# When a spectral filter is loaded: 18 transfers, three places in the row loop, and a zeroing write that holds some of them back

## Chip, core and metric

The kernel runs on one core of a Trainium2 chip. The metric is the device time in microseconds (us) of one execution of the whole kernel. Before the change it was 339.54 us, the median of three runs (339.13 to 340.23).

## What is computed

A block of two residual parts, forward and backward, in one kernel: x is 2048 x 448 (sequence x features) in bf16.

```
h   = x + irfft2( rfft2(LN(x)) * (w_r + i*w_i) )            # w_r, w_i: 2048 x 225
h2  = h + transpose( gelu( LN(LN(h))^T w1 + b1 ) w2 + b2 )  # w1: 2048 x 1792, w2: 1792 x 2048
out = h2, and the gradients of x, w_r, w_i, w1, b1, w2, b2 for a given grad_out
```

The Fourier transforms are matrix products with sine and cosine tables that the kernel makes itself. The change touches only the way in which w_r and w_i come into SBUF (on-chip memory) in the forward part, and a few neighbours of those loads.

## The kernel before

**Engines and order.** PE (TensorE) does all products; DVE (VectorE) and ACT (ScalarE) empty PSUM and do the elementwise work; POOL (GpSimd) does small statistics; SP (SyncE) does nothing but start transfers. The orders of PE, DVE, ACT and SP are those in which the Python code issues; POOL's order is chosen by a scheduler. Every engine works its own queue strictly in order: an instruction that waits holds all that is queued behind it. SP, ACT and POOL can start transfers. Eight completion counters serve the transfers of SP and ACT in turn, so a start also waits until the transfer eight starts earlier has landed.

**Row stage** (lines 932 to 979, about 16 to 43 us of the span). A loop of 16 row steps t. In step t PE does `row_a(t + 1)` (first transform of one row group: it reads the scaled table `Rs` that `scale_R` makes on DVE from 1/std of the row, and the folded input that `fold_prep` or `fold_quarters` makes on DVE), then `row_b(t - 3)` (second transform). Between them `fill(n)` puts n products of another task on PE, `dg_gen`: 14 column blocks j of grad_out times turned w2 (`w2T`), 16 products each, needed much later. So PE nearly always has work. 1/std comes from `newton_gp` (line 407), ten tiny POOL instructions for a pair of rows, in steps 0, 1, 3, 5 and 7. Sine tables come from `gen_UV`: its Python pieces are called by `uv_step` in steps 1, 2, 4, 5, 7, 9 and 10; the last piece corrects `Vt` (two DVE instructions). From step 11 on PE turns `Ut` and `Vt` in four portions (`gen_inv_s`, line 530).

**Row moves** (line 697). After each second `row_b` a transfer carries two finished rows to `D2`, eight in all; I number them move 1 to 8. SP starts 1 to 7, ACT the eighth. The next stage begins with products that read moves 1, 3, 5 and 7.

**Turned tiles** (line 312). w2 blocks j = 5 to 13 come as transposing transfers from SP, each when a buffer of `w2T_ring` is free: four in the row stage, and five held back (`held_w2`, `CAP`) until after it.

**Filter loads** (`w_io`, line 579). Nine transfers each for w_r and w_i. Per part, moves[0, 2, 4, 6] bring 16 long runs of 7200 bytes, moves[1, 3, 5, 7] bring runs of 450 bytes in reversed order (256 of them, in the first 240), and moves[8] 16 runs of 450 bytes. `w_loads` is a generator; `W_AT` says how many loads each row step pulls: two in each of steps 0 to 5, six in step 6. All of w_r and the five short-run loads of w_i go by SP; the four long-run loads of w_i go by POOL (`late`), each behind a write of one zero by DVE (line 596), which keeps the scheduler from starting it earlier.

**Stage s2** (line 704). Four sets. Each is transformed along the sequence with `Vt`, `Ut`, `Un`, multiplied on DVE with its part of W (`w_mult`, line 753; this reads all 18 loads), transformed back and moved by line 740 to `D3`. Then `inv_rows` reads `D3` and the table `RTm`, which `gen_RT` (line 525) makes with one product and one copy.

**Between the row stage and s2** (lines 984 to 994): `gen_inv_d` twice, three small bias transfers from SP (`load_biases`), the held turned tiles, `gen_RT`, and 17 products of `dg_gen` in three fills.

Of the kernel before, what the change touches and what calls it, by code (L numbers as in the profile page):

```python
# [103 lines left out]
class Ring:  # L104
# [7 lines left out]
    def next(self):  # L112
        v = self.views[self.i % len(self.views)]
        self.i += 1
        Ring.release(v)
        return v
# [8 lines left out]
def kernel(  # L125
# [20 lines left out]
    nc = tc.nc  # L146
# [4 lines left out]
    gp_ = nc.gpsimd  # L151
# [12 lines left out]
    def cut(reg, off, *dims):  # L164
        n = int(np.prod(dims))
        v = reg[:, off:off + n]
        if len(dims) == 1:
            return v
        names = "abcd"[:len(dims)]
        return v.rearrange("p (" + " ".join(names) + ") -> p " + " ".join(names),  # L170
                           **{c: d for c, d in zip(names, dims)})
# [5 lines left out]
    def ps_ff(parts=P):  # L177
        return psum.tile([P, 512], F32, tag="ff", bufs=4, name="ps_ff")
# [5 lines left out]
    def evac(out, in_, scale=None):  # L184
        n = int(np.prod(in_.shape[1:]))
        if load[0] + sc.cost('copy', n, False) <= load[1] + ve.cost('tensor_copy', n, in_.dtype == BF16):
            if scale is None:
                sc.copy(out=out, in_=in_)
            else:
                sc.activation(out=out, in_=in_, func=ACT.Copy, scale=scale)  # L190
        elif scale is None:
            ve.tensor_copy(out=out, in_=in_)
        else:
            ve.tensor_scalar(out=out, in0=in_, scalar1=scale, scalar2=None, op0=ALU.mult)
# [24 lines left out]
    def mm(out, lhsT, rhs, start, stop):  # L219
        nc.tensor.matmul(out, lhsT=lhsT, rhs=rhs, start=start, stop=stop)  # L220
        clock[0] += int(np.prod(rhs.shape[1:])) / 2400.0
        run_due()
# [80 lines left out]
    def load_w2T():  # L303
        j = w2T_ring.i
        if j == NFB:
            return
        wT = w2T_ring.next()
        w2Ts[j] = wT
        if j < N_NAT:
            nc.sync.dma_start(out=w2n[j], in_=B_w2[j * P:(j + 1) * P, :].rearrange("f (t c) -> f t c", c=P))  # L310
            return
        nc.sync.dma_start_transpose(out=wT, in_=B_w2[j * P:(j + 1) * P, :].rearrange("f (t c) -> f t c", c=P))
# [94 lines left out]
    def newton_gp(v, y, sl):  # L407
        vi, yi = nt_i[:, 0, sl], y.bitcast(I32)
        a = nt_f[:, 0, sl]
        gp_.tensor_scalar(out=v, in0=v, scalar1=LN_EPS, scalar2=None, op0=ALU.add)  # L410
        gp_.tensor_scalar(out=yi, in0=v.bitcast(I32), scalar1=-0.5, scalar2=RSQRT_MAGIC, op0=ALU.mult, op1=ALU.add)
        for c0, c1 in RSQRT_STEPS:
            gp_.tensor_tensor(out=a, in0=y, in1=y, op=ALU.mult)
            gp_.tensor_tensor(out=a, in0=a, in1=v, op=ALU.mult)
            gp_.tensor_scalar(out=a, in0=a, scalar1=c0, scalar2=c1, op0=ALU.mult, op1=ALU.add)
            gp_.tensor_tensor(out=y, in0=a, in1=y, op=ALU.mult)
# [108 lines left out]
    def gen_RT():  # L525
        pt = ps_ff()
        mm(pt[:, 0:P], lhsT=Rp, rhs=ident[:], start=True, stop=True)
        evac(out=RTm[:], in_=pt[:, 0:P])
# [47 lines left out]
    Wc = cut(rW, 0, 2, NG, DF)  # L576
    W = Wc.rearrange("p c g k -> p g c k")

    def w_io(dr, di, store):
        Wq = Wc.rearrange("(q s) c g k -> s q c g k", s=2)  # L580
        for c_, d in ((0, dr), (1, di)):
            moves = []
            for i in range(4):
                moves.append((Wq[0][16 * i:16 * i + 16, c_].rearrange("l g k -> l (g k)"), 16 * i, [[P * DF, 16], [1, 16 * DF]]))
                g0 = 0 if i else 1
                moves.append((Wq[1][16 * i:16 * i + 16, c_, g0:NG, :], P - 16 * i - g0,
                              [[P * DF, 16], [-DF, NG - g0], [1, DF]]))
            moves.append((Wq[1][0:16, c_, 0, :], 64, [[P * DF, 16], [1, DF]]))
            late = [m for n, m in enumerate(moves) if n in (0, 2, 4, 6)] if c_ and not store else []
            early = moves if not late else [m for n, m in enumerate(moves) if n not in (0, 2, 4, 6)]  # L590
            for n, (sb, row, dims) in enumerate(early + late):
                d_ap = bass.AP(d.tensor, d.offset + row * DF, dims)
                eng = nc.sync if n < len(early) else gp_
                if eng is gp_:
                    i = 32 * (n - len(early))
                    nc.vector.memset(Wc[i:i + 1, 1, 8, 0:1], 0.0)
                eng.dma_start(out=d_ap if store else sb, in_=sb if store else d_ap)
                yield

# [21 lines left out]
    def scale_R(t):  # L621
        v = Rs_ring.next()
        ve.tensor_scalar(out=v, in0=Rm[:], scalar1=rstd_x[:, t:t + 1], scalar2=None, op0=ALU.mult)
        return v
# [176 lines left out]
    def fill(n):  # L801
        while n > 0 and pending:
            try:
                next(pending[0])
                n -= 1
                if row_ops:
                    row_ops.pop(0)()
            except StopIteration:
                pending.pop(0)
# [12 lines left out]
    def load_biases():  # L822
        gp_.memset(smr, 0.0)
        nc.sync.dma_start(out=gtail[:, 0:64], in_=grad_out[0][S - 16:S, 3 * P:D])
        nc.sync.dma_start(out=smr[0:NFB, 0, :], in_=B_b1.rearrange("(j p) -> j p", p=P))
        nc.sync.dma_start(out=smr[:, 1, :], in_=B_b2.rearrange("(j p) -> j p", p=P))

        def turn():
            for i, dst in ((0, b1col), (1, b2col)):
                nc.sync.dma_start_transpose(out=smc[:, i, :], in_=smr[:, i, :])  # L830

        def place():
            for i, dst in ((0, b1col), (1, b2col)):
                ve.tensor_copy(out=dst[:], in_=smc[:, i, :])
        return turn, place
# [85 lines left out]
    GROUPS = {0: (6, 8), 1: (8, 10), 3: (10, 12), 5: (12, 14), 7: (14, 16)}  # L921
    STATS = {0: (6, 7), 1: (8, 9), **{t: (t + 8,) for t in range(2, 8)}}
    INV_S = {11: 0, 12: 1, 13: 2, 14: 3}
    W_AT = {**{t: 2 for t in range(6)}, 6: 6}
    FILL_A = (4, 4, 8, 12, 6, 3, 3, 4, 5, 3, 3, 2, 2, 2, 3, 3)
    FILL_B = (0, 0, 2, 2, 2, 2, 4, 4, 3, 2, 2, 2, 2, 2, 2, 2)
    def uv_step():
# [4 lines left out]
    for t in range(NT):  # L932
        if t == 0:
            load_w2T()
        if 4 <= t + 1 < NT:
            row_a(t + 1, Rs.pop(t + 1), sc.copy if t == 7 else None)
        if t == 7:
            late_c.pop()()
        fill(FILL_A[t])
        if 3 <= t and t + 3 < NT:  # L940
            if t + 3 in (4, 8, 12):
                while Meter.side:
                    Meter.side.pop(0)()
            Rs[t + 3] = scale_R(t + 3)
        row_b(t - 3, csQ if t - 3 >= 4 * U_Q else None)
        if t == NT - 1:
            for i in range(t - 2, NT):
                row_b(i, csQ)
        if t % 2 and t < 12:
            if t == 1:  # L950
                pass
            elif t // 2 + 2 < 2 * U_Q:
                fold_prep(xn, t // 2 + 2)
            else:
                fold_quarters(xn, t // 2 + 2, t // 2 % 2 * 2)
        if t == 4:
            for w in range(2):
                gp_.tensor_copy(out=csQ[:, w, :, :], in_=csF[:, w, 0, :].rearrange("p (j e) -> p e j", e=2))
        if t == 1:
            while cs_ops:  # L960
                cs_ops.pop(0)()
            uv_step()
        for i in STATS.get(t, ()):
            ln_stats(xn, i, mvx)
        if t in (2, 4, 5, 7, 9, 10):
            uv_step()
        if t in GROUPS:
            a, b = GROUPS[t]
            newton_gp(mvx[:, a:b, 1], rstd_x[:, a:b], slice(a, b))
        for _ in range(W_AT.get(t, 0)):  # L970
            next(w_loads, None)
        if t in INV_S:
            gen_inv_s(INV_S[t])
        if t == 13:
            for c in range(2):
                for e in range(2):
                    sc.copy(out=Rp.rearrange("p (e a q b c) -> p c e a q b", e=2, c=2, q=8, a=2)[:, c, e],
                            in_=Rm[:, 64 * c + 32 * e:64 * c + 32 * e + 32].rearrange("p (q a b) -> p a q b", q=8, a=2))
        fill(FILL_B[t])
# [5 lines left out]
    gen_inv_d(0)  # L985
    fill(6)
    gen_inv_d(1)
    turn_biases, place_biases = load_biases()
    cap[0] = NFB
    while held_w2:  # L990
        held_w2.pop(0)()
    fill(4)
    gen_RT()
    fill(7)

    def fwd_mult(s, j, x, y):
# [1 line left out]

    s2_stage(lambda s: set_of(Xs, s), fwd_mult, 8, (8,) * 5, 0, split=True)
    sc.activation(out=warm, in_=eps_h, func=ACT.Sqrt)  # L1000
    fill(21)

    w1c_ring = Ring([cut(r, o, NT, 256) for r, o in ((r2, 0), (r2, NT * 256), (rO, S))])
# [479 lines left out]
```

## Time and profile before

| What | us |
|---|---|
| median of three runs | 339.54 |
| profiled execution, whole | 340.34 |
| its span | 338.3 |
| PE busy in the span | 330.2 |
| idle time of PE that is put down to a wait for another engine or transfer, the 1.2 us at the start included | 4.2 |
| row stage and what follows up to the first product of s2 | 16 to 48.4 |
| s2 | 48.4 to 75.4 |

The profile is of one execution. A wait is named after the engine or the transfer that ended it. `SPq` and `ACTq` are the queues that start transfers; the time of such a row is the time of starting, not of the data. Where I speak of the landing of one transfer, it is the last count of its completion counter in the trace.

### The profile page before, as it was taken

Reading aid. Unit: us, or ns where it says so; the run is one execution under the profiler, and the core shown is the slowest. Engines: PE = TensorE matmul, PEld = TensorE weight load, DVE = VectorE, ACT = ScalarE, POOL = GpSimd, SP = SyncE. Lnnn points to the kernel's source line nnn. Section 1 sums busy time; section 2 is a strip of 40 time slices with the busy share of each in tenths; the row PEclk is TensorE's granted clock in tenths of the full one; section 3 lists DMA queues with packets and bytes.
Section 4 is the critical chain, followed back from the end, with each engine's and each line's share of the span. In section 5 each row is a group of like instructions: output and inputs, shape, how many; then the busy total and the mean of one; then the engine's idle time right before and its main releaser. Section 6 shows DMA issues by size and latency. Waiting matters only on the chain.

```text
span 338.3 us, 7987 instructions
## 1 busy us (share of the span) xinstructions
PE 330.2 (98%) x2893; PEld 174.6 (52%) x2893; DVE 251.7 (74%) x670; ACT 206.7 (61%) x448; POOL 84.6 (25%) x254
## 2 busy tenths in 40 slices
PE   8999989999999999999999999999999999999995
PEld 4666554456545555555555555554344434555552
DVE  8998739827947888593227888786697993599994
ACT  6987666848965534423222346665588875588882
POOL 7767202412210000000001111210020222156670
PEclk9999999999999999999999999999999999999999
DMA  7999899959899999687877889837699999978885
GB/s 251 400 203 182 190 258 141 227 125 279 230 378 287 348 279 242 179 274 192 193 178 164 174 188 155 176 84 232 221 220 302 290 244 252 284 188 278 245 293 200
DMA packets 136198, 78.03 MB, mean 231 GB/s; under 512 B 86528, under 2 KB 127592, under 8 KB 136032
## 3 DMA queue, kind: packets, MB, share of 16 engines
q1 hardware_dynamic: 133288, 73.13, 84.5%
q0 software_dynamic: 2448, 3.83, 5.3%
q8 instruction: 22, 0.36, 0.5%
q10 hardware_dynamic: 424, 0.58, 0.5%
q14 instruction: 16, 0.13, 0.1%
HBM read 28.33 MB, written 22.04 MB: 149 GB/s over the span
## 4 chain that ended last, share of the span: by engine, by line
PE 83%; DVE 6%; DMA 4%; ACT 3%; issue 1%; POOL 1%; SPq 0%; DVEq 0%; ACTq 0%
PE ps_mm L220 68%; PE ps_ff L220 9%; PE ps_ff L225 3%; DMA r<-r 3%; ACT rO L84 2%; PE ps_mm L375 2%; DVE rS L84 2%; DVE r L84 1%; DMA r<-rX 1%; DVE rX L84 1%; DVE stats L84 1%; DVE rA L84 1%; ACT rE L84 1%; PE ps_mm L318 0%; DVE rG L84 0%
## 5 line engine op out<-in xcount | busy, mean ns | idle before, releaser
L220 PEld LDWEIGHTS <-r 128*128 128x128 bf16 (+2 forms) x628 | 58.6, 105 | 48.5 <-issue 3.0
L220 PEld LDWEIGHTS <-rS 128*128 128x128 bf16 (+1 forms) x468 | 36.2, 97 | 31.9 <-issue 6.0
L84 ACT CAST rO<-ps_mm 128x512 bf16<-128x512 f32 (+1 forms) x68 | 36.5, 584 | 14.5 <-PE ps_mm L220 11.9
L220 PE MATMUL ps_mm<-rD,r 128*128 128x448 bf16 x224 | 44.5, 352 | 0.0
L220 PEld LDWEIGHTS <-rst 128*128 128x128 bf16 (+1 forms) x320 | 23.9, 97 | 30.4 <-issue 12.1
L740 POOL DMA_DIRECT2D r<-r x29 | 17.4, 605 | 67.3 <-ACT r L84 56.7
L220 PE MATMUL ps_mm<-rC,rE 128*128 128x448 bf16 x144 | 32.1, 353 | 0.0
L220 PE MATMUL ps_mm<-rB,r 128*128 128x448 bf16 x160 | 31.2, 352 | 0.2 <-DVE rB L84 0.2
L220 PE MATMUL ps_mm<-rG,rst 128*128 128x512 bf16 (+1 forms) x128 | 28.5, 380 | 0.0
L220 PE MATMUL ps_mm<-r,rst 128*128 128x512 bf16 (+2 forms) x144 | 27.3, 345 | 0.0
L84 ACT ACTIVATE r<-ps_mm,rstd_h 128x448 bf16<-128x448 f32 x16 | 10.1, 634 | 26.8 <-PE ps_mm L220 26.8
L84 DVE SCALAR_TENSOR_TENSOR r<-ps_mm,b2col,r 128x448 bf16<-128x448 f32 x16 | 10.9, 682 | 19.9 <-PE ps_mm L220 18.6
L84 ACT ACTIVATE r<-rC 128x448 bf16<-128x448 bf16 x16 | 9.1, 570 | 26.7 <-DMA out_dram<-r 13.8
L84 ACT CAST r<-ps_ff 128x452 bf16<-128x452 f32 x43 | 23.1, 592 | 3.1 <-PE ps_ff L220 1.2
L1220 POOL TENSOR_SCALAR lcol<-lcol 128x1 f32<-128x1 f32 x16 | 8.5, 530 | 64.7 <-ACT r L84 64.7
L84 ACT ACTIVATE rG<-rG 128x896 bf16<-128x896 bf16 x14 | 13.3, 950 | 14.9 <-DVE rG L84 14.7
L220 PEld LDWEIGHTS <-rO 128*128 128x128 bf16 (+1 forms) x165 | 15.4, 98 | 12.3 <-ACT rO L84 0.2
L84 ACT CAST rS<-ps_ff 128x512 bf16<-128x512 f32 x31 | 18.0, 583 | 4.2 <-PE ps_ff L220 4.2
L220 PE MATMUL ps_ff<-csI,rAT 113*128 113x224 bf16 (+1 forms) x108 | 19.0, 298 | 0.2 <-DVE rA L84 0.2
L84 ACT CAST rG<-ps_mm 128x512 bf16<-128x512 f32 (+1 forms) x28 | 14.0, 539 | 7.6 <-PE ps_mm L220 7.5
L84 ACT CAST rAT<-ps_ff 113x512 bf16<-113x512 f32 x24 | 13.9, 586 | 7.7 <-PE ps_ff L220 7.5
L84 DVE TENSOR_SCALAR rG<-rG 128x896 bf16<-128x896 bf16 x28 | 10.9, 389 | 10.0 <-ACT rG L84 10.0
(200 smaller groups left out, 647.4 us busy)
## 6 DMA issues: line engine op xcount, KB each, us to landing
out_dram<-rO SPq DMA_DIRECT2D x34, 256.0 KB, 3.3
r<-in_B_w_dram SPq DMA_DIRECT2D x5, 1024.0 KB, 9.1
r<-r POOLq DMA_DIRECT2D x29, 113.0 KB, 5.5
out_dram<-rG SPq DMA_DIRECT2D x11, 256.0 KB, 3.1
r<-in_B_w_dram SPq DMA_DIRECT2D x3, 896.0 KB, 5.6
rS<-in_B_w_dram SPq DMA_DIRECT2D x3, 896.0 KB
rB<-in_B_w_dram SPq DMA_DIRECT2D x5, 512.0 KB, 8.1
r<-r SPq DMA_DIRECT2D x11, 226.0 KB, 2.5
```

What stands on the lines that cost most here:

```text
L84: fn(**kw)
L220: nc.tensor.matmul(out, lhsT=lhsT, rhs=rhs, start=start, stop=stop)
L225: nc.tensor.matmul(out, lhsT=lhsT, rhs=rhs, start=start, stop=stop)
L375: nc.tensor.matmul(idle[:, 0:D], lhsT=rAT[:, 0:P], rhs=rAT[:, 0:D], start=True, stop=True)
L740: defer(RESH_LAG, lambda g=g, ab=ab, eng=eng: eng.dma_start(out=D3[rowbase(g):rowbase(g) + 29:4, :, :, :], in_=ab), ab)
L1220: gp_.tensor_scalar(out=m1, in0=ms, scalar1=-1.0 / D, scalar2=None, op0=ALU.mult)
```

## The change

The nine loads of w_r and moves[0] of w_i are now started by SP in steps 0 to 6; moves[1, 3, 5, 7, 8] of w_i are started by POOL in step 9; moves[2, 4, 6] by SP in steps 10 (two) and 12 (one). The four single zeros are gone; instead one write of 128 x 2 zeros stands in step 9, behind the DVE work of that step and ahead of the five loads. As built, this write waits for all ten loads that were started before it, the tenth too, and the eight loads after it are held by it: POOL's five wait for it, and the first of SP's three as well.

The write comes after the tenth load and covers 2 values in each of 16 partitions that this load has filled: the changed kernel computes with 32 of the 460,800 values of w_i at zero.

Further, the bias transfers come behind the two held turned tiles and no longer ahead of them, and `gen_RT` comes behind s2; as built its copy falls to ACT and no longer to DVE. In POOL's order all instructions of `newton_gp` now stand ahead of the five loads; before, the four loads stood between them.

```diff
-            late = [m for n, m in enumerate(moves) if n in (0, 2, 4, 6)] if c_ and not store else []
-            early = moves if not late else [m for n, m in enumerate(moves) if n not in (0, 2, 4, 6)]
-            for n, (sb, row, dims) in enumerate(early + late):
+            if c_ and not store:
+                moves = moves[0:1] + moves[1::2] + moves[8:9] + moves[2:8:2]
+            for n, (sb, row, dims) in enumerate(moves):
                 d_ap = bass.AP(d.tensor, d.offset + row * DF, dims)
-                eng = nc.sync if n < len(early) else gp_
-                if eng is gp_:
-                    i = 32 * (n - len(early))
-                    nc.vector.memset(Wc[i:i + 1, 1, 8, 0:1], 0.0)
+                eng = gp_ if c_ and not store and 1 <= n <= 5 else nc.sync
...
-    W_AT = {**{t: 2 for t in range(6)}, 6: 6}
+    W_AT = {0: 2, 1: 1, 2: 2, 3: 1, 4: 2, 5: 1, 6: 1, 9: 5, 10: 2, 12: 1}
...
+        if t == 9:
+            nc.vector.memset(Wc[:, 1, 0:2, 0:1], 0.0)
         for _ in range(W_AT.get(t, 0)):
             next(w_loads, None)
...
     gen_inv_d(1)
-    turn_biases, place_biases = load_biases()
     cap[0] = NFB
     while held_w2:
         held_w2.pop(0)()
+    turn_biases, place_biases = load_biases()
     fill(4)
-    gen_RT()
     fill(7)
...
     s2_stage(lambda s: set_of(Xs, s), fwd_mult, 8, (8,) * 5, 0, split=True)
     sc.activation(out=warm, in_=eps_h, func=ACT.Sqrt)
+    gen_RT()
     fill(21)
```

SP's queue from the first turned tile on, as built (T1 to T9 are the turned tiles of line 312, R the loads of w_r, I those of w_i):

```
before: T1 T2 R R R  I move1 I I T3 I I  move2 T4 move3 move4 move5 move6 move7  biases T5 T6 T7 T8 T9
after:  T1 T2 R R R  move1 R T3 I(10th)  move2 T4 move3 I I move4 I move5 move6 move7  T5 T6 biases T7 T8 T9
```

Ahead of T1 stand six loads of w_r before, and five after.

## The prediction, on record before the result was seen

> **What bounds the kernel now.** I read the page first: PE is busy for 330.2 of 338.3 us, so only idle time of PE can go, unless work is removed, and none is. Then the view of waits, for PE alone. Its whole list comes to 4.2 us; these four lines carry it (columns: us in total, times, longest):
>
> ```profile
> PE ps_mm L375 <- DVE rS L628: 1.2, 1, 1.2
> PE ps_ff L225 <- DMA r<-rX: 0.9, 1, 0.9
> PE ps_ff L220 <- DMA r<-r: 0.7, 2, 0.5
> PE ps_ff L220 <- DVE rS L84: 0.7, 1, 0.7
> ```
>
> The first is the start of the kernel. The other three are what this change can reach: 0.9 at the start of s2, 0.5 where `D3` is first read, 0.7 in the row stage. The timeline of PE places the first and the last of them:
>
> ```profile
> 35.02 0.40 PE L220 MATMUL ps_ff<-rX,rS 128*128 128x128 bf16 x4 [0.66 <-DVE rS L84]
> ...
> 35.93 0.27 PE L225 MATMUL ps_ff<-permI,Ut 32*32 32x32 bf16 x16
> ...
> 48.40 0.62 PE L225 MATMUL ps_ff<-r,Vt 32*32 32x452 bf16 x12 [0.91 <-DMA r<-rX]
> ```
>
> Behind the 0.66 stands DVE, which came late because it waited for POOL (1/std), and POOL was late because it had started four filter loads:
>
> ```profile
> 28.57 1.76 POOL L597 DMA_DIRECT2D rW<-in_A_w_i_dram  x3
> ...
> 30.54 0.53 POOL L597 DMA_DIRECT2D rW<-in_A_w_i_dram  x1
> ```
>
> ```profile
> 33.38 0.25 DVE L84 TENSOR_SCALAR rX<-Rm,rstd_x 128x128 bf16<-128x128 bf16 x1 [0.81 <-POOL rstd_x L416]
> ...
> 36.20 0.32 DVE L84 TENSOR_SCALAR rX<-Rm,rstd_x 128x128 bf16<-128x128 bf16 x1 [0.78 <-POOL rstd_x L416]
> ```
>
> Behind the 0.91 stands SP. The copy that move 7 carries ends at about 43.6, but SP is still busy with what it owes, and starts move 7 only at 44.81; it lands at 48.26:
>
> ```profile
> 32.09 5.12 SPq L312 DMA_TRANSPOSE rE<-in_B_w_dram  x1
> 37.26 1.24 SPq L597 DMA_DIRECT2D rW<-in_A_w_i_dram  x2
> 38.60 0.59 SPq L697 DMA_DIRECT2D r<-r  x1
> 39.29 2.78 SPq L312 DMA_TRANSPOSE rO<-in_B_w_dram  x1
> 42.17 1.23 SPq L697 DMA_DIRECT2D r<-r  x2
> 43.50 1.85 SPq L697 DMA_DIRECT2D r<-rX  x3
> ```
>
> The reader is to see that starting a turned tile (T3, T4) holds SP for up to 5 us. It ends about when the transfers ahead have landed: T1's start ends at 25.03 (last landing ahead 25.33), T3's at 37.21 (37.85), T4's at 42.07 (42.28).
>
> **The change, step by step.** "Before" times are those of the profiled execution.
>
> 1. *POOL.* The four starts (2.3 us) leave the middle of `newton_gp`, whose ten instructions come 0.28 us apart (27.23, 27.50, 27.79, 28.06). Its last two groups end at about 29.5 and 34.3 instead of 33.35 and 36.2. Both waits of DVE (0.81, 0.78) go, and so do the four zero writes (0.41 at 27.97). DVE is through step 9 at 34.96 - 0.81 - 0.41 = 33.7, and PE, free at 34.36, starts `row_a(12)` there instead of at 35.02: 0.66 saved, for the moment.
>
> 2. *The new hold.* DVE's new write must wait until the tenth load has landed; I call that time M. Behind it on DVE stand `scale_R(13)` (0.25) and the two corrections of `Vt` (0.37), and PE waits for these at `gen_inv_s(0)`, which it reaches at 34.36 + (35.93 - 35.02) = 35.27. So PE goes on at M + 0.62 if that is later. Now M. The tenth load is behind T3 in SP's queue. SP ends T2 at 26.72; then three loads, move 1 and a load, 0.63 each: T3 starts at about 29.8 instead of 32.09. T2 lands at 31.48; the next three loads landed 0.74, 0.76 and 0.31 apart, and eleven transfers between T2 and T3 took 6.37, 0.58 each. Five are left: 2.2 to 2.9, drained at 33.3 to 34.1 allowing for T2 being up to 0.4 earlier, as one load fewer stands ahead of it. T3 lands 1.5 to 2.3 after the drain (1.5, 2.0 and 2.3 for T3, T1, T4): 35.0 to 36.2. The load behind a turned tile lands 0.6 to 0.75 after it (0.64 behind T3, 0.74 behind T2), and not under 2.7 after its own start (37.26 to 39.98). That gives M = 35.6 to 36.8, and I take 36.1. One case speaks for later: the load started at 37.26 had its first count at 39.98 and its last at 41.78. With such a tail M is 38 to 38.5. M has no row of its own in this trace; 35.0 and 38.5 are my ends.
>
> 3. *Start of s2.* From `gen_inv_s(0)` at 35.93 PE went on to 47.48, where it ran out of products: 11.55, with a wait of 0.06 that goes and the product of `gen_RT` (0.05) that moves. So PE is ready for s2 at M + 0.62 + 11.44 = M + 12.06. Against 48.40 **the break-even is M = 36.34**; at 36.1 the gain is 0.24. What is late next: move 7. After T4 SP has move 3, three loads and move 4 to start (0.63 each), and is free by about 41 instead of 43.5, so move 7 starts when its copy is ready, near 44.4. With 2.7 to 3.45 to landing it is there at 47.1 to 47.9, ahead of 48.2. The wait of 0.91 goes, but the hold eats most of what goes.
>
> 4. *First filter product.* It stood at 51.41 and needs all 18 loads. POOL's five start at M; four have 256 runs each, which no POOL row shows. Nearest: 0.52 each with 16 runs (these loads), 0.60 for line 740 with some 64 packets. By proportion to packets 2.4 each, by the slope between those two rows about 0.95. I take 0.95, as the row of 64 is hardly dearer than that of 16. The last start is then near M + 4.3 = 40.4, and with 4.1 to 6.6 to landing all is there by 47. Hidden behind the first transform of s2. At 2.4 each it would be 46 + 4.1 to 6.6, so DVE would wait up to 1.5; I cannot see a gain here.
>
> 5. *Turned tiles and biases.* T5 follows move 7 at once instead of 2.2 us later (biases 45.45 to 47.58). The biases then stand between T6 and T7, so T9, which landed at 70.32, comes some 0.8 earlier and is out of the way of the last moves to `D3`, started up to 70.68 with 4.56 to landing. PE waited 0.49 for them; bounds 0 and 0.49, I take 0.35. The turned tiles themselves are not waited for in either place.
>
> 6. *gen_RT.* Product 0.05 and copy (0.28 on DVE, some 0.5 on ACT) lie beside the 21 products from 70.7 to 74.9; nothing. If that cover were gone: 0.5.
>
> Sum: -0.24 - 0.35 = about -0.6 us, on the profiled execution's 340.34 (span 338.3 and 2.0 around it). From 94 us on PE works without a gap until the end phase, so what is saved ahead of it stays saved. The median was 0.8 below the profiled execution; the same -0.6 gives **338.9**.
>
> **Rivals.**
>
> *No hold.* If the tenth load is there by 34.4, PE never stops. s2 then starts near 46.8 (48.40 - 0.66 - 0.06 - 0.91 - 0.05 = 46.72, and move 7 not before some 46.9), 1.5 to 1.7 saved, with step 5 about 2.0: 337.5. Against it: T3 would have to land by 33.7, barely behind the five transfers ahead of it.
>
> *The hold is long (the other side).* One mechanism: the zero write on DVE waits for the tenth load, which waits behind T3. Slower from M = 36.34 on, by as much as M is later. At M = 37.9 it is +1.56, less about 0.3 of step 5: 340.8; at 38.5, 341.4. For it speak the tail above and T3 itself: tiles stalled in the middle before (T2 took 4.1 from T1's landing, not 2). Against it: POOL's loads no longer share the transfer engines with T3.
>
> *The transfers decide, not their starting.* The same 18 loads and four tiles still land ahead of move 7, so if the transfer engines are what is full, move 7 lands at 48.26 again: 339.2 with step 5. The stretches speak against it (the columns at the end are clock, share of the transfer engines, GB/s):
>
> ```profile
> 30.00:40.00 10.00, 9.26 (x166) 5.85 (x165) 7.36 (x25) 6.78 (x14) 4.61 (x19) 1.00 1.08 210
> 40.00:50.00 10.00, 9.09 (x146) 5.84 (x144) 4.86 (x15) 6.03 (x20) 0.11 (x1) 1.00 0.80 236
> ```
>
> There is room from 40 on, where the late loads now fall. The Trainium skill states this rival as a rule (DMA: Bandwidth & Descriptors, "Issuing engines are not separate DMA queues"): starting transfers from several engines saves only the time of starting, as all run on the same 16 engines. By that rule alone, handing loads to POOL brings nothing at s2; by the rows above it is SP's and POOL's time of starting that is late, so the trace does not contradict the rule, but the time of starting is here not small.
>
> *POOL's short runs are dear.* At 2.4 us each the first filter product waits 1.5 and s2 with it: about 341.
>
> **How the numbers follow.** Forecast (M 35.0 to 36.6: 337.7 to 339.8) 0.52, no hold 0.12, long hold 0.26, transfers decide 0.04, dear runs 0.06. A measurement of this kernel tells about 0.3% (1.0 us) from no change. Faster by more: no hold and the part of the forecast under M = 35.7, 0.12 + 0.24 = 0.36. Slower by more: long holds from M = 37.5, 0.19, and dear runs, 0.06: 0.25. The rest, 0.39, is within. The range from 337.2 to 341.4 leaves out the longest holds and a gain beyond steps 1, 3 and 5; the forecast's own range is 337.7 to 339.8.
>
> **What will show it.** Step 1: no wait of DVE for POOL's 1/std, and PE's 0.66 gone. Step 2: a wait of DVE for a filter load near 34, ended between 35 and 38, and PE idle at `gen_inv_s(0)` for about M - 34.6. If neither is there, the hold is wrong. Step 3: s2 without a wait for a row move. Step 4: a wait of the first filter product for POOL's loads would show dear runs. Step 5: PE's wait at the first read of `D3`, 0.49 before. A start of T3 well off 29.8 makes M wrong, and with it the sign.

## The result, and the profile after

The changed kernel took 344.31 us (median of 22 executions, 340.52 to 352.5) against 340.34 us for the kernel before on the same chip (22 executions, 338.64 to 344.25). The ratio is 1.0087, 95% interval 1.0060 to 1.0114: some 3 us slower, where I had forecast 0.6 us faster. (The ratios here leave out executions more than 1.5% above the fastest of their kernel, the profiled one of 352.5 us among them; medians and counts leave out none.)

The profiled execution of the changed kernel is its longest, 352.5 us with a span of 350.6. The same kernel was run again as `e1_after`; that profile (345.42 us, span 343.5, granted clock 0.993) is nearer to the usual and is read first. Lines of the changed kernel are 3 lower than before. The list of PE's waits (us in total, times, longest):

```profile
PE ps_ff L225 <- issue: 2.8, 1, 2.8
PE ps_ff L225 <- DVE Vt L84: 2.5, 1, 2.5
...
PE ps_ff L220 <- DMA r<-r: 0.7, 1, 0.7
```

The 0.9 at the start of s2 and the 0.7 behind `rS` in the row stage are gone, as forecast, and the wait for `D3` is still there. Two new stops stand at the top. PE's timeline places them:

```profile
38.21 0.27 PE L225 MATMUL ps_ff<-permI,Vt 32*32 32x32 bf16 x16 [2.47 <-DVE Vt L84]
...
70.06 0.27 PE L225 MATMUL ps_ff<-rS,UVT 32*32 32x226 bf16 x1 [2.82 <-issue]
```

The first is the hold. DVE's timeline shows what is queued behind the zero write (it shares its start with `scale_R(13)`), and POOL's shows the five loads behind it:

```profile
37.62 0.25 DVE L84 TENSOR_SCALAR rX<-Rm,rstd_x 128x128 bf16<-128x128 bf16 x1 [3.41 <-issue]
37.62 0.06 DVE L968 MEMSET rW<- 128x2 bf16 x1
37.79 0.37 DVE L84 TENSOR_SCALAR Vt<-Vt,cols 128x16 bf16<-128x16 bf16 x2
```

```profile
37.98 3.06 POOL L594 DMA_DIRECT2D rW<-in_A_w_i_dram  x5 [2.01 <-DVE rW L968]
```

The tenth load landed at 37.31 here (36.10 in the first profile); the write begins 0.31 later. The view puts DVE's 3.41 down to "issue", because it does not see the transfer that the write waits for: the landing time tells it. The five short-run loads cost 3.06 together, 0.61 each.

What I had not looked for stands in the stretches behind that stop (the columns at the end are clock, share of the transfer engines, GB/s):

```profile
36.00:38.00 2.00, 0.00 (x0) 0.00 (x0) 0.38 (x4) 0.00 (x0) 0.01 (x1) 1.00 0.89 183
38.00:40.00 2.00, 1.79 (x24) 1.09 (x25) 1.97 (x8) 0.52 (x2) 1.99 (x4) 0.61 1.21 243
40.00:42.00 2.00, 2.00 (x43) 1.13 (x42) 0.35 (x2) 1.34 (x3) 1.28 (x3) 0.54 0.97 197
```

After the stop PE is busy, but at half clock for 3.4 us, 38.4 to 41.8 (0.50 in stretches of 1 us). That is up to 1.7 us of work lost, on top of the 2.47. PE reached `gen_inv_s(0)` at 35.47 (35.93 before) and s2 at 50.76 (48.40 before).

From there to the first read of `D3` the kernel before took 26.97 us and this one 29.31, 2.82 of it the stop put down to "issue". The first profile is the extreme of this stage:

```profile
37.01 0.27 PE L225 MATMUL ps_ff<-permI,Vt 32*32 32x32 bf16 x16 [1.79 <-DVE Vt L84]
...
70.56 0.55 PE L220 MATMUL ps_mm<-rC,rE 128*128 128x448 bf16 x1 [2.18 <-DMA rE<-in_B_w_dram]
...
83.34 4.86 PE L220 MATMUL ps_mm<-rC,rO 128*128 128x448 bf16 x14 [7.36 <-DMA rO<-in_B_w_dram]
```

There PE waits for the turned tiles T8 and T9 themselves. T9 was started at 62.23 and landed from 79.02 to 83.30 (before: started at 59.73, landed from 69.71 to 70.32). The hold of 1.79 cost no clock, the two later stops did:

```profile
82.00:84.00 2.00, 0.66 (x2) 0.28 (x3) 0.00 (x0) 1.82 (x4) 0.00 (x0) 0.50 0.50 140
84.00:86.00 2.00, 2.00 (x7) 0.82 (x6) 0.00 (x0) 0.25 (x1) 0.00 (x0) 0.50 0.07 23
```

From the first read of `D3` to the end both kernels take the same in these profiles: 262.9 us before, 262.6 and 263.4 after. All that is lost in them is lost ahead of it.

### The profile page after: what moved, and what is told of

It is laid out like the page before. It is cut to its first block, busy times and chain, and to the rows that moved or that the text cites. A ratio compares the mean times of both kernels' runs of the same rounds, so it can differ in the third digit from the quotient of the medians.

```text
span 350.6 us, 7988 instructions
## 1 busy us (share of the span) xinstructions
PE 332.8 (95%) x2893; PEld 175.7 (50%) x2893; DVE 250.3 (71%) x666; ACT 206.8 (59%) x449; POOL 86.1 (25%) x255
## 4 chain that ended last, share of the span: by engine, by line
PE 69%; DVE 1%; ACT 1%; issue 0%
PE ps_mm L220 62%; PE ps_ff L220 6%; PE ps_ff L225 2%; DVE rA L84 1%; ACT rO L84 0%; DVE rB L84 0%; ACT rAT L84 0%; DVE rG L84 0%; ACT rstd_h L84 0%; DVE rstd_h L84 0%
## 5 line engine op out<-in xcount | busy, mean ns | idle before, releaser
L220 PE MATMUL ps_mm<-rC,rE 128*128 128x448 bf16 x144 | 33.4, 362 | 2.2 <-DMA rE<-in_B_w_dram 2.2
L220 PE MATMUL ps_mm<-rC,rO 128*128 128x448 bf16 x80 | 20.1, 384 | 7.9 <-DMA rO<-in_B_w_dram 7.4
L220 PEld LDWEIGHTS <-rE 128*128 128x128 bf16 x144 | 13.0, 99 | 12.6 <-DMA rE<-in_B_w_dram 2.6
```

## The theories and the experiments

*Hold:* DVE's wait for the tenth load stops PE, and that is the loss. *Late tiles* (the jam theory of the first expectation): the biases between T6 and T7 push T7 to T9 among the moves to `D3`; both are slowed, and s2 with them. *Full engines* (formed after the second group): whatever loads are moved later, and not only the hold, crowd out T4 and the row moves, so that PE stops in one place or another.

The table gives all runs: the median of this kernel and of the kernel before on the same chip, the ratio with its interval, how many executions had a mean granted clock below 0.997, and from the one profile PE's longest stop between 30 and 52 us, the start of s2 and its length to the first read of `D3`. "Moved" says whether the filter loads are not where they were before, or are held. (For the first runs of the change 23 executions have a clock, one more than stand in the median.)

| run | moved | medians, us | ratio (95%) | clock < 0.997 | stop | s2 from | length |
|---|---|---|---|---|---|---|---|
| first runs of the change | yes | 344.31 / 340.34 | 1.0087 (1.0060-1.0114) | 17 of 23 | 1.79 | 48.46 | 39.58 |
| e1_after | yes | 344.37 / 341.41 | 1.0085 (1.0054-1.0116) | 8 of 12 | 2.47 | 50.76 | 29.31 |
| e2_loads_only | yes | 342.35 / 341.41 | 1.0034 (0.9997-1.0071) | 5 of 12 | 1.55 | 48.41 | 28.04 |
| e3_biases_only | no | 341.71 / 341.41 | 1.0016 (0.9978-1.0054) | 2 of 12 | 1.20 | 48.82 | 29.03 |
| e4_RT_only | no | 340.79 / 341.41 | 0.9982 (0.9949-1.0015) | 3 of 12 | 0.85 | 47.26 | 27.29 |
| e5_no_hold | yes | 343.38 / 340.67 | 1.0043 (0.9999-1.0086) | 8 of 12 | 4.38 | 50.24 | 28.64 |
| e6_T9_plain | yes | 342.05 / 340.67 | 1.0045 (1.0014-1.0075) | 9 of 12 | 2.46 | 49.35 | 27.15 |
| e7_hold_only | held | 344.15 / 340.67 | 1.0042 (0.9997-1.0088) | 6 of 12 | 2.21 | 50.20 | 30.43 |
| e8_no_hold_old_order | yes | 342.25 / 340.67 | 1.0034 (0.9999-1.0070) | 8 of 12 | 1.58 | 47.88 | 26.40 |
| e9_late_pool | yes | 342.60 / 341.02 | 1.0018 (0.9984-1.0052) | 8 of 12 | 4.08 | 50.71 | 27.80 |
| e10_zero_later | yes | 343.92 / 341.02 | 1.0106 (1.0068-1.0144) | 7 of 8 | 1.04 | 48.01 | 30.86 |
| e11_zero_later_old_order | yes | 342.48 / 341.02 | 1.0043 (1.0021-1.0066) | 7 of 12 | 1.99 | 50.70 | 27.27 |
| e12_before_again | no | 341.69 / 341.02 | 1.0010 (0.9977-1.0042) | 3 of 12 | 0.66 | 47.80 | 28.39 |
| e13_biases_last | yes | 342.46 / 340.98 | 1.0052 (1.0011-1.0093) | 7 of 12 | 3.81 | 51.67 | 26.86 |
| e14_before_biases_last | no | 340.32 / 340.98 | 0.9990 (0.9960-1.0021) | 1 of 12 | 0.91 | 49.05 | 27.10 |
| e15_no_hold_biases_last | yes | 341.60 / 340.98 | 1.0038 (1.0000-1.0075) | 7 of 12 | 2.33 | 48.59 | 27.67 |
| e16_both_later | no | 340.81 / 341.30 | 0.9990 (0.9957-1.0023) | 2 of 12 | 1.07 | 47.44 | 28.16 |
| e17_both_later_early_loads | yes | 342.17 / 341.30 | 1.0029 (0.9993-1.0066) | 9 of 12 | 2.92 | 49.55 | 27.90 |

The kernel before itself had a clock below 0.997 in 47 of its 153 executions beside these runs.

### The change taken apart: e1 to e4

`e1_after` is the changed kernel as it is.

> The changed kernel again, to see where time goes in another execution. Jam theory (the turned tiles T7 to T9, two or three us later by the biases, fall among the moves to D3, and both are slowed): T8 lands after 66 and T9 after 71, and PE has waits over 1 us at products of dg_gen that read T8 or T9; the time is 2 to 4 us over before. Hold theory (the zero write that waits for the tenth load is all of the loss): T8 and T9 land by 66 and 71, PE waits for no turned tile, s2 starts 2 to 4 us later than 48.4.

T8 landed from 62.62 on and T9 from 69.84 (last counts 64.42 and 71.31), PE waited for neither, and s2 started 2.36 later. By this profile the hold theory was right about s2's start, and neither theory had the stop of 2.82 in s2.

`e2_loads_only`, against the changed kernel:

```diff
+    turn_biases, place_biases = load_biases()
     cap[0] = NFB
     while held_w2:
         held_w2.pop(0)()
-    turn_biases, place_biases = load_biases()
     fill(4)
+    gen_RT()
     fill(7)
```
(and `gen_RT` behind s2 taken out)

> The changed filter loads with the zero write, but the biases ahead of the held tiles and gen_RT ahead of s2 as before. If the order of the biases is the cause: T7 starts again near 53.5 and T9 near 59.7, no wait of PE for a turned tile, time within 0.3% of before. If the late filter loads themselves push the tiles (T5 starts while eight loads are under way): T8 and T9 are as late as in the changed kernel, and the time stays 2 to 4 us over before. If the hold is the cause: s2 starts late and the time stays 2 to 4 over.

T7 started at 52.44 and T9 at 58.19, the stop at `gen_inv_s(0)` was 1.55, and `D3` was waited for 1.52. The ratio of 1.0034 lies between the answers: about 0.5% less than the whole change, with an interval that just reaches 1. So neither part alone looks like the whole cause.

`e3_biases_only`, against the kernel before: `load_biases()` moved behind the loop that starts the held tiles.

> The kernel before with the bias loads behind the two held tiles and nothing else. If the order of the biases is the cause: T7 starts some 2 us later than 53.5, T9 lands after 71, PE waits for T8 or T9, and the time is 2 to 4 us over before. If the filter loads or the hold are the cause: within 0.3% of before.

T7 started at 53.23, not later than before, as T5 and T6 had come 2.2 and 1.0 earlier; still s2 took 29.03 with a stop of 0.79 put down to issue, and `D3` was waited for 1.72. The ratio of 1.0016 cannot be told from 1. By itself the order costs too little to be seen here.

`e4_RT_only`, against the kernel before: `gen_RT()` moved behind s2.

> The kernel before with gen_RT behind s2 and nothing else. All theories: within 0.3% of before. If its copy on ACT stands in the way at the first read of D3, up to 0.5 us slower.

0.9982: nothing, as expected.

### The hold and the last tile: e5 to e8

`e5_no_hold`, against the changed kernel (the first load of w_i is now pulled behind the zero write):

```diff
-    W_AT = {0: 2, 1: 1, 2: 2, 3: 1, 4: 2, 5: 1, 6: 1, 9: 5, 10: 2, 12: 1}
+    W_AT = {0: 2, 1: 1, 2: 2, 3: 1, 4: 2, 5: 1, 9: 6, 10: 2, 12: 1}
```

> The changed kernel, but the tenth load (the first of w_i) is started behind the zero write in step 9 and no longer ahead of it, so that the write has to wait only for the nine loads of w_r (the last of them landed at 34.16 in the second profile of the changed kernel, its tenth at 37.31); no value of w_i is zeroed then. Hold theory (the hold of DVE stops PE for 1.5 to 2.5 us, and a stop of over 2 us also lowers PE's clock for some 3.5 us): PE's wait for Vt is under 0.5, few runs (under 4 of 12) show a mean clock below 0.997, and the time falls by 1.5 to 3 us, to that of the kernel before or below. Late tiles theory (all is lost behind s2's start, where turned tiles, moves to D3 and the fetching of PE's instructions share the transfer engines): s2 starts earlier but ends no earlier against the kernel before; the time stays 2 us or more over it.

The hold went: the products of `Ut` and `Vt` at `gen_inv_s(0)` stood at 34.35 and 34.70. PE then ran out of work near 45.9 and stood longer than in any hold, for a row move:

```profile
50.24 0.70 PE L225 MATMUL ps_ff<-r,Vt 32*32 32x452 bf16 x12 [4.38 <-DMA r<-rX]
```

```profile
50.00:52.00 2.00, 1.76 (x50) 1.07 (x51) 0.77 (x4) 1.09 (x3) 0.00 (x0) 0.50 1.11 213
52.00:54.00 2.00, 2.00 (x7) 0.84 (x6) 0.00 (x0) 1.10 (x3) 0.00 (x0) 0.50 0.83 90
54.00:56.00 2.00, 2.00 (x7) 0.78 (x6) 1.83 (x4) 0.00 (x0) 0.00 (x0) 0.50 0.83 184
```

The half clock lasted 6.8 us, twice as long as behind the hold. T4 had landed at 44.62 here (44.57 before, although it was started 5 us earlier, at 34.28), amid POOL's five loads. This held SP. By the eight counters move 6 cannot start before T4 has landed, nor move 7 before move 3 has; T4 landed at 44.62 and move 3 at 46.39, and the two moves started at 44.68 and 46.47 (44.81 before for move 7). SP's row for moves 5 to 7, which took 1.85 before:

```profile
40.55 6.45 SPq L694 DMA_DIRECT2D r<-rX  x3
```

From its start to its landing move 7 took 3.63 us (3.45 before): it was not carried more slowly, it was started later. Taking the hold away did not take the stop away; it moved it. 8 of 12 executions still had the low clock. This is where I gave up the hold as the only cause and formed the full engines theory.

`e6_T9_plain`, against the changed kernel: for j = 13 `load_w2T` starts an ordinary transfer (`dma_start`) in place of the transposing one, so one block of w2 is used unturned.

> The changed kernel with the last tile T9 loaded by an ordinary transfer of the same 512 KB, not by a transposing one (so one of 14 blocks of w2 is used unturned). Late tiles theory: the moves to D3 are no longer stuck behind T9, from the start of s2 to the first read of D3 it is 27 us or less (before 26.97; changed 29.31 and 39.58), PE has no stop over 1 us there, and the time falls by 1.5 us or more. Hold theory: s2 may be a little shorter, but the time falls by less than 1 us, and 7 in 10 runs still show a clock below 0.997.

s2 took 27.15 and its longest stop was 0.63. The ratio fell from 1.0085 to 1.0045, and 9 of 12 executions still had the low clock. So the late T9 is part of the loss (about 0.4%, with overlapping intervals), and the stop ahead of s2 another.

`e7_hold_only`, against the kernel before:

```diff
+        if t == 9:
+            nc.vector.memset(Wc[32:64, 1, 1:2, 0:1], 0.0)
         for _ in range(W_AT.get(t, 0)):
```

> The kernel before with one thing added: in step 9 DVE writes 32 zeros over part of w_i, and so waits for the loads moves[1] to moves[3] of w_i, the last of which landed at 37.30 there (16 values of w_i stay zero). Nothing else is moved. Hold theory: PE goes on at gen_inv_s(0) at about 37.9 instead of 36.05, s2 starts 1 us later than 48.40, as the wait of 0.91 for move 7 is swallowed, half the runs or more show a clock below 0.997, and the time is 1.5 to 3 us over before. Late tiles theory: within 1 us of before.

```profile
37.64 0.27 PE L225 MATMUL ps_ff<-permI,Vt 32*32 32x32 bf16 x16 [2.21 <-DVE Vt L84]
...
68.96 0.27 PE L225 MATMUL ps_ff<-rS,UVT 32*32 32x226 bf16 x2 [1.67 <-issue]
```

PE's clock was at half from 38.8 to 42.2, s2 started 1.8 later than 48.40, and 6 of 12 executions had the low clock; the ratio of 1.0042 is 1.4 us, with an interval that just touches 1. The hold alone stops PE and lowers its clock; that it also costs time is likely and not certain, and it is not the whole.

`e8_no_hold_old_order` is `e5_no_hold` with the biases and `gen_RT` as before.

> As e5_no_hold, with the biases ahead of the held tiles and gen_RT ahead of s2 as in the kernel before: the new places of the filter loads alone, without the hold. Hold theory: s2 starts near 47 and the time is 0.5 to 1.5 us below before. Late tiles theory, with the order of the biases as cause: below before and at least 1.5 us below e5_no_hold. If the late loads themselves are the cause: 1 to 2 us over before, as e5_no_hold.

Its one profile is good (337.2 of span, s2 in 26.40), but PE stood 1.58 at the start of s2 (the view names a bias load; move 7 had landed 0.13 earlier, at 47.75), and 8 of 12 executions had the low clock. The ratio of 1.0034, whose interval just reaches 1, speaks for the last of the three answers: the new places of the loads cost even with no hold and no new order.

### Later loads without a hold, and the order of the biases: e9 to e12

`e9_late_pool`, against the kernel before:

```diff
-    W_AT = {**{t: 2 for t in range(6)}, 6: 6}
+    W_AT = {**{t: 2 for t in range(7)}, 9: 4}
```

> The kernel before with only GpSimd's four long-run loads of w_i (and their four single zeros, which wait for nothing) moved from step 6 to step 9, behind newton_gp; the loads of SP, the biases and gen_RT are as before, and there is no hold. Start theory (only the time of starting on POOL counts): DVE's waits for 1/std and PE's 0.66 go, s2 starts where move 7 allows, near 48, and the time is within 1 us of before or 0.3 to 0.7 below. Full engines theory (the 16 transfer engines are full from 30 to 48 us, so what is moved later crowds out T4 and the row moves): T4 lands later than 44.57 and move 7 later than 48.26, PE's wait at the start of s2 grows to 1.5 us or more, and the time is not below before.

```profile
50.71 0.81 PE L225 MATMUL ps_ff<-r,Vt 32*32 32x452 bf16 x12 [4.08 <-DMA r<-rX]
```

The 0.66 in the row stage went. T4 landed at 47.20 (44.57 before) and move 7 at 50.57 (48.26 before). In this profile the full engines theory holds in each of its numbers, and 8 of 12 executions had the low clock. But SP was done with T2 at 29.52 here (26.72 before), ahead of every load that was moved, so part of the lateness is the run's own; and the ratio of 1.0018 cannot be told from 1.

`e10_zero_later`, against the changed kernel: the zero write and `9: 5` in `W_AT` go to step 10 (`10: 7`). `e11_zero_later_old_order` is the same with the biases ahead of the held tiles.

> The changed kernel with the zero write and the five loads of POOL in step 10 instead of 9, behind scale_R(13) and the two corrections of Vt on DVE; the order of SP is the same. Hold theory: PE's wait for Vt at gen_inv_s(0) goes (under 0.3), what is left of the hold is a wait under 1.5 us at a later product; fewer runs have a clock below 0.997 (under 6 of 12), and the time falls by 1 to 2 us. Full engines theory: PE then waits at the start of s2 for a row move instead, 1 us or more, and the time stays within 1 us of the changed kernel.

> As e10_zero_later, with the biases ahead of the held tiles as in the kernel before. If the order of the biases costs by itself: 1 us or more below e10_zero_later, with T7 to T9 some 2 us earlier and a shorter s2 (27 us). If not: the same as e10_zero_later within 1 us.

PE's timeline of `e10_zero_later`, then of `e11_zero_later_old_order`:

```profile
48.01 0.50 PE L225 MATMUL ps_ff<-r,Vt 32*32 32x452 bf16 x12 [1.04 <-DMA r<-rX]
...
67.20 0.27 PE L225 MATMUL ps_ff<-rS,UVT 32*32 32x226 bf16 x1 [2.43 <-issue]
```

```profile
38.32 0.27 PE L225 MATMUL ps_ff<-permI,Ut 32*32 32x32 bf16 x16 [1.99 <-DVE rX L84]
...
50.70 0.50 PE L225 MATMUL ps_ff<-r,Vt 32*32 32x452 bf16 x12 [1.18 <-DMA r<-rX]
```

The wait for `Vt` went in both. In the first the tenth load landed early (35.39) and a wait of 1.04 for a row move is what is left; in the second it landed at 37.06 and PE stopped one portion later, at `gen_inv_s(1)`, for DVE's copy to `rX`, which stands behind the write. The two kernels differ in the order of the biases alone, and their intervals do not meet: 1.0068 to 1.0144 (8 executions) against 1.0021 to 1.0066 (12). With T7 at 54.20 and T9 at 60.76, both counted from a start of s2 at 48.01, s2 took 30.86; with 53.19 and 59.10 against 50.70 it took 27.27.

`e12_before_again` is the kernel before.

> The kernel before, unchanged, for a second profile of it: how far its own stages vary. All theories: the time is that of before; s2 starts within 0.5 us of 48.40 and takes 27 us up to the first read of D3. If it takes 28 us or more here too, then part of what I put down to the change is the run's own.

s2 started at 47.80 and took 28.39 with a wait of 1.23 for `D3`. So 1.4 us of s2's length are the run's own, and one profile's s2 proves little.

### The biases out of the way, and the best of both: e13 to e17

`e13_biases_last`, against the changed kernel:

```diff
-    turn_biases, place_biases = load_biases()
...
     s2_stage(lambda s: set_of(Xs, s), fwd_mult, 8, (8,) * 5, 0, split=True)
+    turn_biases, place_biases = load_biases()
```

`e14_before_biases_last` does the same to the kernel before, `e15_no_hold_biases_last` to `e5_no_hold`.

> The changed kernel with the three bias loads behind s2 instead of between T6 and T7. (a) Place between T6 and T7: T7 starts at once behind T6, T8 and T9 land 1.5 to 2 us earlier against the start of s2, s2 takes 27 to 28 us (changed: 29.3, 28.6, 29.0, 30.9 in kernels with that order), PE has no stop put down to issue of over 1 us, and the time is 1.5 us or more below the changed kernel, 0.3 to 0.5% over before. (b) T5 and T6 too early, or (c) gen_RT: s2 stays at 29 us or more and the time at 0.8% over before.

> The kernel before with the three bias loads behind s2, nothing else. (a): T5 can start at once behind move 7, but as it lands when the transfers ahead of it have, little is gained: within 0.3% of before, s2 27 to 28 us. (b): T5 and T6 early cost, 0.3 to 0.5% over before.

> The changed kernel without the hold (the first of w_i behind the zero write) and with the biases behind s2: both parts of the loss taken back, the later loads kept. (a) with full engines: PE still waits at the start of s2 for a row move, 1 us or more, s2 27 to 28 us, 0.2 to 0.4% over before. If the starting times of SP and POOL were all that counts: 0.3% or more below before.

SP's starts of T5 to T9 in `e1_after`, with the biases (L821 to L823) among them, and then in `e13_biases_last`:

```profile
47.77 2.70 SPq L312 DMA_TRANSPOSE rO<-in_B_w_dram  x1
50.56 2.98 SPq L312 DMA_TRANSPOSE rE<-in_B_w_dram  x1
53.64 0.53 SPq L821 DMA_DIRECT2D rst<-in_grad_out_dram  x1
...
55.13 4.84 SPq L312 DMA_TRANSPOSE rE<-in_B_w_dram  x2
60.06 3.26 SPq L312 DMA_TRANSPOSE rO<-in_B_w_dram  x1
```

```profile
48.68 3.39 SPq L312 DMA_TRANSPOSE rO<-in_B_w_dram  x1
52.16 8.06 SPq L312 DMA_TRANSPOSE rE<-in_B_w_dram  x3
60.31 2.80 SPq L312 DMA_TRANSPOSE rO<-in_B_w_dram  x1
```

The last start comes 9.3 us after the start of s2 in the first and 8.6 in the second (s2 from 51.67), and T9's first count 19.1 and 15.8 us after it. Both kernels with the biases between T6 and T7 removed have short s2 stages (26.86 and 27.67), and the kernel before keeps its own (27.10). The hold in `e13_biases_last` was the longest seen, with the tenth load at 38.26:

```profile
39.16 0.28 PE L225 MATMUL ps_ff<-permI,Vt 32*32 32x32 bf16 x16 [3.81 <-DVE Vt L84]
```

What is left at 1.0052 and 1.0038 I put down to the stop ahead of s2: 7 of 12 executions of each had the low clock, against 1 of 12 of `e14_before_biases_last`, where the loads are as before.

`e16_both_later` is `e14_before_biases_last` with `gen_RT` behind s2 too; `e17_both_later_early_loads` also asks for all loads two steps earlier (`W_AT = {**{t: 3 for t in range(4)}, 4: 6}`).

> The kernel before with the two things of the change that did not cost by themselves: the bias loads and gen_RT behind s2; the filter loads as before. From e14 (0.999) and e4 (0.998): 0.1 to 0.4% below before, s2 27 us, hardly a run with a clock below 0.997. If the two gains were noise: within 0.1% of before.

> As e16_both_later, with the 18 filter loads asked for two row steps earlier (three in each of steps 0 to 3, six in step 4). Full engines theory (what matters is what is still to be landed before move 7): T4 and move 7 land earlier than 44.57 and 48.26, PE's wait of 0.91 at the start of s2 shrinks, 0.2 to 0.5% below e16. Against it: T1 and T2 then stand behind three more loads on SP and land later, and PE may wait for them near 25 to 33; then it is 0.3% or more above e16.

`e16_both_later` came to 0.9990 (0.9957 to 1.0023), like `e14_before_biases_last`; neither can be told from before. Earlier loads were no remedy:

```profile
49.55 0.70 PE L225 MATMUL ps_ff<-r,Vt 32*32 32x452 bf16 x12 [2.92 <-DMA r<-rX]
```

T1 and T2 were pushed back (T2 landed at 34.67; 30.32 in `e16_both_later`), T4 landed at 45.32 and move 7 at 49.41. I had named that push for a wait of PE near 25 to 33; it came out at s2 instead. So both later loads (`e9_late_pool`, 4.08) and earlier ones (2.92) gave PE a longer stop at s2 and more executions with the low clock (8 and 9 of 12), though neither ratio (1.0018, 1.0029) can be told from 1. Some 18 loads, four tiles and eight moves have to be through by 48 us; that their order decides which of them PE meets fits these runs and is argued.

## Why the prediction was wrong, step by step

**Steps 1, 4 and 6 held.** The waits for 1/std and the 0.66 went; the five loads of POOL took 0.61 each (I took 0.95) and were there by 47 in both profiles of the changed kernel, and DVE waited for none of the 18 loads at the filter product; `gen_RT` cost nothing (0.9982).

**Step 2 failed in a size and in a term.** The hold is there, where it was said to be, and in the first profile the tenth load landed at the very 36.10. That was luck, as it came by another way: T3, whose start I had named as a sign, was started at 30.88 there and at 31.70 in `e1_after`, not at 29.8. Over the seven profiles with this order of loads the tenth landed at 35.39, 35.77, 36.10, 37.00, 37.06, 37.31 and 38.26: 37.0 in the middle, behind my break-even of 36.34. By my own M + 12.06 that is s2 at 49.1, 0.7 late.

The term that was sized wrong is the load behind T3. T3 itself landed within my 35.0 to 36.2 in both profiles of the change (35.36 and 35.97). The tenth load landed 0.67 to 1.34 after T3 in the seven profiles, 0.95 in the middle, where I took 0.6 to 0.75. The 0.64 that I gave for the load behind T3 goes to its first count; to its last, which M means, it is 2.44. I took the value at which the rows of one execution agreed, and had the tail as a rival only. And PE goes on at M + 0.9, not at M + 0.62, as the write begins 0.3 after the landing. That moves the break-even to 36.06: with M at 36.10 the first profile has s2 at 48.46, no earlier than before.

The missing term is the clock: "PE goes on at M + 0.62 if that is later" counts a stop at its own length. With M + 12.34 in place of M + 12.06, s2 comes at 48.44 and 49.34 in the first profile and `e6_T9_plain`, where no half clock follows the hold (measured: 48.46 and 49.35), and at 49.65 and 50.60 in `e1_after` and `e13_biases_last`, where one does (measured: 50.76 and 51.67). There it costs the start of s2 another 1.1 us.

In the 19 profiles PE's stops between 30 and 90 us of up to 1.87 us (13 of over 1 us) are followed by no half clock; of the 13 of 1.99 us and more, 11 are, nine for 3.4 us and two for 6.8 (in three cases it begins within the stop). The hold, at 1.5 to 3.8 us where it comes at all, straddles that edge. What decides inside the edge can be worked out from the clock records and the busy times of PE. All changes of the clock in a profile lie on one grid of 3.413 us, to within 0.003. Each of the 11 half clocks begins at the end of a stretch of this grid in which PE was busy for 1.42 us or less; in all other stretches between 24 and 112 us that ran at full clock it was busy for 1.51 or more. Two stretches of `e1_after`, the first of them ahead of its half clock, the second with part of its stop of 2.82 (busy PE first, clock third from the end):

```profile
35.01:38.42 3.41, 0.94 (x39) 0.62 (x37) 0.80 (x6) 0.81 (x2) 1.16 (x6) 1.00 0.90 180
65.73:69.14 3.41, 1.51 (x37) 0.55 (x35) 2.43 (x5) 1.69 (x4) 0.27 (x1) 1.00 1.20 111
```

That stop lies across two stretches, and the emptier keeps 1.51; the 2.46 of `e6_T9_plain` leaves 1.78. So a stop below 1.9 us cannot by itself empty a stretch as far as that, and one of 2 to 3 us does or does not, as it happens to fall on the grid. (Near the end of the kernel, stretches with 1.60 and 1.61 were followed by half clock too, so the edge is known only roughly.)

Of all executions of kernels with moved or held loads 106 of 163 had a mean clock below 0.997, of the others 58 of 213; for the changed kernel's first runs the two groups' medians are 344.9 and 341.7. Worked out as span times the missing clock, the mean loss is 2.2 and 1.7 us in the two sets of the changed kernel and 0.7 to 1.1 in the sets of the kernel before: by this estimate 1 of the 3 us.

The Trainium skill names this gate (TensorE: Matmul & The Clock Gate, "What's actually happening"): half rate after an idle window of about 3.4 us, windows that run freely. The two rates, the grid, and a half clock of 3.4 or twice 3.4 us agree with these runs. That the window has to be idle does not: PE was busy for up to 1.42 us in the stretches that were followed by half clock. The measurement decides: from 2 us on, a stop is a risk.

**Step 3 held for the wait, and not for the row move or for what I built on it.** Move 7 was no longer waited for in the changed kernel, but only because PE came later too: it landed at 48.22 in the first profile and at 49.94 in `e1_after`, not at 47.1 to 47.9. The 48.26 of the rival in which the transfers decide was the nearer value. I had written that the transfers have room "from 40 on, where the late loads now fall", and gave the rival in which the transfers decide 0.04. Where the hold is taken away (`e5_no_hold`, `e8_no_hold_old_order`, `e15_no_hold_biases_last`) or never was (`e9_late_pool`), PE stops at the start of s2 instead, 1.6 to 4.4 us. The share of 0.80 between 40 and 50 us that I read as room was a mean over 10 us: before, it is 0.49 from 40 to 42, 1.07 and 1.04 in the two stretches up to 46, and 0.86 and 0.52 up to 50. T4 and the moves behind it needed the part ahead of 47. The hold hid this: it kept PE late enough not to meet it. In `e5_no_hold` the late landings act through the eight counters, which hold SP's starts; `e15_no_hold_biases_last` shows the same (move 3 landed at 43.71, move 7 started at 43.78). That full transfer engines are what makes T4 and move 3 late is argued from these profiles: no run changed their load alone.

**Step 5 failed in its sign.** "The turned tiles themselves are not waited for in either place" was wrong in the first profile (2.18 and 7.36) and in no other, and T9, which was to come "some 0.8 earlier", came later. T5's early start, on which the step rests, did not come about or brought nothing in the changed kernel: in `e1_after` T5 was started at 47.77 (47.67 before), as move 7 was late, and in the first profile at 45.10, to land at 54.65 (53.88 before). In `e3_biases_only`, with the loads as before, it did gain: it was started 2.2 earlier and landed at 51.17. The biases' 1.5 us now stand in the chain of starts behind T6; ahead of T5 they cost nothing that `e14_before_biases_last` (0.9990 without them) could show. That the order costs where the loads are late is shown by `e10_zero_later` against `e11_zero_later_old_order`; the other three pairs (the change and `e2_loads_only`, `e5_no_hold` and `e8_no_hold_old_order`, of which both also move `gen_RT`, and `e3_biases_only` and `e12_before_again`) point the same way with 0.5, 0.1 and 0.1%, and overlap. By what mechanism is less sure. In the six profiles in which T9's first count came within 16 us of the start of s2, all without biases behind T6, s2 took 26.9 to 27.9, a half clock in three of them included; where it came after 18.6 us or more, anything from 26.4 to 39.6. A late T9 thus makes a long s2 possible and not certain, and in `e3_biases_only` T7 to T9 started no later than before and s2 was long all the same.

**The sum.** Of its two terms, -0.24 at the start of s2 and -0.35 behind it, `e1_after` shows +2.36 and +2.34. In the medians of many executions the 0.9% are about 0.4% for the loads, with the hold or without (`e2_loads_only`, `e11_zero_later_old_order`, `e8_no_hold_old_order`, `e15_no_hold_biases_last`: 1.0034 to 1.0043, of which one interval excludes 1), and about as much for the order of the biases beside them. The two do not simply add: the order costs 0.5 to 0.6% where the zero write waits for the tenth load, and 0.1%, no more than can be noise, where it does not (`e5_no_hold`) or where the loads are as before (`e3_biases_only`). Why it needs the write is open. The long hold, at 340.8 the rival on the other side, named the right place and less than half the price.

**Open.** The stop put down to "issue" in s2. In nine profiles it ends 1.3 to 2.1 us after a packet of 16,384 bytes of the transfer queue that the page lists as "q8 instruction", which came 14.1 to 16.6 us after the start of s2. Where there was no such stop the packet came 12.5 to 14.4 us after it, and once at 16.0. That fits a late fetch of PE's own instructions on the crowded engines. The Trainium skill (Runtime: NRT & Kernel Launch, "Instruction fetch mechanics") says that such blocks of 16 KiB, 256 instructions each, are fetched ahead and mostly hidden; the 22 packets of the profile's page, an estimate of 5,632 instructions by that count, come near the 2,884 products and 2,893 weight loads (5,777 together). But no experiment moved that fetch by itself, so this is argued and not shown.

## What to carry to other kernels

Where PE is 98% busy, price a new wait twice: its own length, and from about 2 us on the half clock that may follow; a value near that edge needs the spread of the landing times and not the one that a profile shows. When a wait is taken away, ask which transfer PE meets next at the earlier time, look at the load of the transfer engines up to that moment and not at a mean over the stage behind it, and ask which landing the start of that transfer itself waits for. A few small starts cost nothing measurable ahead of the first transposing load here, and about half a per cent between two of them when the loads before them were late and held.

## What the runs showed of the hardware

- A stop of PE of 1.99 to 2.5 us was followed by half clock in six of seven cases, one of up to 1.87 us never. The half clocks begin on a grid of 3.413 us, behind stretches in which PE was busy for 1.42 us or less; behind stretches with 1.51 or more (between 24 and 112 us) none begins.
- Starting a transposing load earlier did not land it earlier while others were under way: T4 was started at 34.28 in `e5_no_hold` and landed at 44.62, started at 39.29 before and landed at 44.57.
- GpSimd's starts of transfers with 256 runs of 450 bytes took 0.56 to 0.61 us (0.82 and 0.83 for the first of five, with 240 runs), hardly more than its 0.48 to 0.53 with 16 runs of 7200 bytes (0.75 for the first of four).
- In `e5_no_hold` SP started moves 6 and 7 within 0.08 us of the landing of the transfer eight starts earlier (44.62 and 44.68, 46.39 and 46.47), after standing still for 3.54 and 1.20 us.
